# An attention and expert kernel on one core: the rounding of the expert's weights moves from POOL to DVE, and the additions for the last 64 keys move from POOL to DVE from the sixth double pair on

## The chip, the cores and the metric

The kernel runs on one core of a Trainium2 chip. The metric is the time of one execution on the device in microseconds (us); the kernel before has a median of 554.97 us over 3 runs (554.33 to 555.19). The engines are called as in the profile: PE does the matrix products and PEld loads their weights, DVE is the vector engine, ACT computes tanh and exp, POOL is the general-purpose engine (it also issues indirect DMAs), and SP issues the other DMAs.

## The reference, cut to what matters

```python
def _attn_ref(q, k, v, cap):                 # q, k, v: 8 x 12 x 448 x 64, float32
    scores = q @ k.transpose / sqrt(64)
    scores = cap * np.tanh(scores / cap)
    scores = scores - max(scores)
    attn = np.exp(scores); attn = attn / (sum(attn) + 1e-09)
    return attn @ v

def _moe_ref(x, w_gate, w1, w2, capacity):   # x: 8 x 448 x 768; w1: 768 x 1024; w2: 1024 x 768
    scores = x @ w_gate
    out = x.copy()
    for b in range(8):
        top_idx = the 128 rows of x[b] with the highest scores
        xe = x[b, top_idx]
        ye = np.maximum(xe @ w1, 0.0) @ w2
        out[b, top_idx] = xe + sigmoid(scores[b, top_idx]) * ye
```

## The kernel before

**Work and order.** Attention is done in 24 double pairs (class `Double`, number `d`, 0 to 23): four heads of one batch element, three double pairs for each of the 8. A double pair is seven steps, each 128 keys of one pair of heads, except the step `(None, 3)`, which holds the last 64 keys of both pairs: pair 0 in partitions 0 to 63 of its tile `pl`, pair 1 in partitions 64 to 127. Two steps make a block of the main loop in `fast_path`. In a block PE forms the scores of the two new steps (line 225, tile `ps`), ACT turns them into `p` or `pl` by tanh and exp (lines 241 and 242), and PE multiplies the two steps of the block before by `v` into the accumulators `x` (pair 0) and `y` (pair 1) (lines 258 and 262). On PE, ACT, DVE and POOL the instructions run in the order in which the program writes them; the SP queue is ordered by a scheduler, with the loads of `q`, `k` and `v` given a priority, and runs in that order.

**The row sums.** `e_step` adds the three 128-key tiles of a pair on DVE into `e` (lines 277 and 279) and then adds the half of `pl` that belongs to the pair, 64 partitions by 896 elements, on POOL (line 283). Once both pairs of a double pair are through, four matrix products with ones (line 291) sum `e` over the keys. DVE copies the sums to `sm` (line 294), PE transposes them (319), DVE makes the reciprocals `rec` (322, 325). `take_x` copies an accumulator to `xT` right behind `e_step` (line 270), PE transposes it (334), and DVE multiplies it by `rec` into `xn` (338), which SP stores and which DVE reduces with `w_gate` to scores (`jk`, line 351).

**Selection and expert.** After each third double pair DVE ranks the scores of the batch element (lines 381 to 421, among them line 393, which counts ties), POOL gathers the 128 chosen rows, and the expert's products (lines 505 and 525) are put between the attention blocks. The transposes of all these steps and the expert's accumulators share two banks, `pt` and `ph`. Each block runs on DVE in this order: what the block before deferred (`sm`, `rec`, `xn`), then `e_step` and `take_x`, then scores and ranking, then one step of the weights' generator.

**The weights.** The expert multiplies in split precision: each weight is a rounded part (`w1h`, `w2h`) and a rest (`w1l`, `w2l`). `weights_gen` makes them once, early in the program, in 14 chunks, 6 of w1 (128x1024) and 8 of w2 (128x768), through three staging buffers (`hs` and two called `stage`). In the kernel before, POOL rounds a chunk (line 183) and DVE subtracts one block later (line 177); the subtraction frees the buffer, and the DMA on SP that loads the next chunk into it (line 167) waits for it. A DMA issued behind it on SP waits with it.

Of the kernel before, what the change touches and what calls it, by code (L numbers as in the profile page):

```python
# [8 lines left out]
F32 = mybir.dt.float32  # L9
# [4 lines left out]
ALU = mybir.AluOpType  # L14
# [7 lines left out]
WARM = 3  # L22
BUDGET = 2500
TAIL = 1500
EVAC, SPLIT = 1300, 2200
HALF = (slice(0, HD), slice(HD, 2 * HD))

# [127 lines left out]
def weights_gen(tc, K, w1, w2):  # L155
    nc = tc.nc
    parts = [(nm, w, i, m) for nm, w, n, m in (("w1", w1, K.ND, K.F), ("w2", w2, K.NF, K.DM))
             for i in range(n)]
    staged = []

    def load(n):
        nm, w, i, m = parts[n]
        if n % 3 == 0:
            st = K.hs
        else:
            st = K.work.tile([P, 1024], F32, tag=("mh", "ml")[n % 3 - 1], name="stage", bufs=1)
        nc.sync.dma_start(st[:, :m], w[i * P:(i + 1) * P, :])
        staged.append(st)

    for n in range(3):  # L170
        load(n)
    yield
    for n in range(len(parts) + 1):
        if n:
            nm, w, i, m = parts[n - 1]
            hi, lo = K.wts[nm + "h"], K.wts[nm + "l"]
            nc.vector.tensor_tensor(lo[:, i, :], staged[n - 1][:, :m], hi[:, i, :].bitcast(F32),
                                    op=ALU.subtract)
            if n + 2 < len(parts):
                load(n + 2)  # L180
        if n < len(parts):
            nm, w, i, m = parts[n]
            nc.gpsimd.tensor_copy(K.wts[nm + "h"][:, i, :], staged[n][:, :m])
        yield


# [86 lines left out]
def e_step(tc, K, D, h, c):  # L273
    nc = tc.nc
    if c == 1:
        D.E[h] = K.work.tile([P, 2, K.S], F32, tag="E", name="e", bufs=3)
        nc.vector.tensor_tensor(D.E[h], D.P[h, 0], D.P[h, 1], op=ALU.add)  # L277
    elif c == 2:
        nc.vector.tensor_tensor(D.E[h], D.E[h], D.P[h, 2], op=ALU.add)  # L279
    if (h, c) in (D.order[3], D.order[6]):  # L280
        i = int((h, c) == D.order[6])
        e, pl = D.E[i], D.P[None, 3]
        nc.gpsimd.tensor_tensor(e[HALF[i]], e[HALF[i]], pl[HALF[i]], op=ALU.add)  # L283


def sums_mm(tc, K, D):
# [352 lines left out]
def fast_path(tc, K, first, wgen):  # L639
# [33 lines left out]
    while u <= nblocks or sums or fill.busy() or any(K.queues.values()):  # L673
# [14 lines left out]
        for s in old:  # L688
            if s:
                e_step(tc, K, *s)  # L690
                take_x(tc, K, *s)
# [13 lines left out]
        if not K.tail:  # L705
# [16 lines left out]
            if not new[0]:  # L722
                K.t += TAIL
        else:
            end = K.t + TAIL
            fill.expert(TAIL)
            K.t = max(K.t, end)
# [8 lines left out]
def main_kernel(ctx: ExitStack, tc: tile.TileContext, q, k, v, cap, w_gate, w1, w2, out, C, dims):  # L736
# [23 lines left out]
    with tc.If(fast > 0) as cmp:  # L760
        engines = {mybir.EngineType.PE, mybir.EngineType.Activation, mybir.EngineType.DVE,
                   mybir.EngineType.Pool}
        with tc.manual_schedule(engines=engines) if C <= P else nullcontext():
            fast_path(tc, K, first, weights_gen(tc, K, w1, w2))
    with cmp.Else():
        load_consts(tc, K)
        for _ in weights_gen(tc, K, w1, w2):
            pass
        general_path(tc, K)
# [47 lines left out]
```

## Time and profile before

| | |
|---|---|
| median of 3 runs | 554.97 us (554.33 to 555.19) |
| profiled execution | 556.0 us, of which 554.2 us lie between its first and its last instruction (the span) |
| PE busy | 513.5 us, 93% of the span, mean granted clock 0.988 |
| DVE busy | 352.2 us (64%) |
| ACT busy | 360.4 us (65%) |
| POOL busy | 139.2 us (25%) |

Busy time is an average over stages that are bound by different engines. Until about 98 us the weights are prepared beside the attention; from there to about 500 us attention and expert run together; the rest is the last batch element's selection and expert, one step after the other. In the profile an instruction that waits inside the engine counts as busy, so a group whose mean lies far above its least time was held up while it ran.

### The profile page before, as it was taken

The numbers are of one execution on the slowest core, as the hardware profiler recorded it, in microseconds if no ns is written. First come the engines' busy times: TensorE is split into PE (matmuls) and PEld (weight loads), VectorE is DVE, ScalarE is ACT, GpSimd is POOL, SyncE is SP. The second block draws the span as 40 slices with busy tenths as digits, with TensorE's granted clock in tenths as the row PEclk, the third lists the DMA queues.
The fourth block names the chain that finished last, engine by engine and source line by source line (L and its number), as shares of the span: only waits on it lengthen the run. The fifth ranks groups of instructions, "written<-read, shape, count | busy, mean of one in ns | idle before, by whom it ended". The sixth has DMA issues, their size and how long they took to land.

```text
span 554.2 us, 8869 instructions
## 1 busy us (share of the span) xinstructions
PE 513.5 (93%) x3446; PEld 260.4 (47%) x3446; DVE 352.2 (64%) x775; ACT 360.4 (65%) x394; POOL 139.2 (25%) x88
## 2 busy tenths in 40 slices
PE   5889989999999999999899998999999998988994
PEld 2223323354544445444454455545454454626884
DVE  1799999757636557665865565854865644865611
ACT  4987976976667574876657775686666866560110
POOL 1565532413212130431122311231313221130000
PEclk9998999999999999999999999999999999998898
DMA  7546653423214231632232331432323412212100
GB/s 256 190 156 190 193 163 119 125 86 101 74 55 149 81 100 39 186 101 84 82 108 85 114 118 34 127 130 67 99 85 107 135 47 87 67 57 69 29 30 34
DMA packets 32034, 57.63 MB, mean 104 GB/s; under 512 B 2944, under 2 KB 25984, under 8 KB 31984
## 3 DMA queue, kind: packets, MB, share of 16 engines
q1 hardware_dynamic: 30704, 50.69, 29.6%
q0 software_dynamic: 1280, 6.29, 3.4%
q8 instruction: 29, 0.48, 0.4%
q14 instruction: 21, 0.17, 0.1%
HBM read 42.81 MB, written 14.16 MB: 103 GB/s over the span
## 4 chain that ended last, share of the span: by engine, by line
PE 69%; DVE 17%; issue 5%; ACT 3%; DMA 2%; POOL 1%; POOLq 0%; DVEq 0%; SPq 0%
PE ps L225 20%; PE ph L525 9%; PE y L262 8%; PE ph L505 8%; PE x L262 8%; DVE jk L351 4%; PE pt L334 3%; PE x L258 3%; PE pt L291 3%; DVE jk L393 2%; DVE e L277 2%; DVE e L279 2%; DVE xT L270 2%; ACT p L241 2%; PE pt L472 2%
## 5 line engine op out<-in xcount | busy, mean ns | idle before, releaser
L241 ACT ACTIVATE p<-ps,sc 128x896 f32<-128x896 f32 x144 | 143.4, 996 | 73.2 <-PE ps L225 61.2
L283 POOL TENSOR_TENSOR e<-e,pl 64x896 f32<-64x896 f32 x48 | 100.5, 2093 | 288.5 <-DVE e L279 235.1
L225 PE MATMUL ps<-q,k 64*64 64x448 f32 x1344 | 150.8, 555 | 6.3 <-DMA k<-in_k 3.5
L242 ACT ACTIVATE p<-p,capc 128x896 f32<-128x896 f32 x144 | 150.2, 1043 | 4.7
L225 PEld LDWEIGHTS ps<-q,k 64*64 64x64 f32 x1344 | 43.5, 133 | 71.0 <-issue 45.8
L262 PE MATMUL y<-p,v 128*64 128x448 f32 x288 | 64.9, 556 | 0.1
L262 PE MATMUL x<-p,v 128*64 128x448 f32 x288 | 64.9, 558 | 0.0
L277 DVE TENSOR_TENSOR e<-p 128x896 f32<-128x896 f32 x48 | 59.8, 1246 | 6.6 <-ACT p L242 6.6
L279 DVE TENSOR_TENSOR e<-e,p 128x896 f32<-128x896 f32 x48 | 53.3, 1111 | 5.4 <-ACT p L242 3.8
L351 DVE CUSTOM_DVE_ANT_0 jk<-xn,wg 112x256 bf16<-112x256 f32 x96 | 51.2, 534 | 2.9
L338 DVE TENSOR_TENSOR xn<-pt,rec 112x512 f32<-112x512 f32 x39 | 26.9, 690 | 26.8 <-PE pt L334 26.2
L241 ACT ACTIVATE pl<-ps,sc 128x896 f32<-128x896 f32 x24 | 24.1, 1003 | 29.1 <-PE ps L225 28.7
L270 DVE COPY xT<-x 128x448 f32<-128x448 f32 x24 | 15.0, 623 | 39.6 <-PE x L262 25.3
L262 PEld LDWEIGHTS x<-p,v 128*64 128x64 f32 x288 | 17.7, 138 | 43.4 <-issue 31.6
L262 PEld LDWEIGHTS y<-p,v 128*64 128x64 f32 x288 | 16.3, 135 | 44.8 <-issue 31.9
L525 PE MATMUL ph<-w2h,hh 128*128 128x384 f32 x112 | 27.6, 359 | 0.0
L242 ACT ACTIVATE pl<-pl,capc 128x896 f32<-128x896 f32 x24 | 25.0, 1042 | 0.8
L505 PE MATMUL ph<-w1l,xh 128*128 128x512 f32 x84 | 25.1, 409 | 0.0
L334 PE MATMUL pt<-ident,xT 128*112 128x128 f32 x156 | 24.4, 279 | 0.7 <-DVE rec L322 0.7
L511 ACT ACTIVATE hs<-ph 128x512 f32<-128x512 f32 x14 | 8.4, 598 | 25.5 <-PE ph L505 25.3
L525 PE MATMUL ph<-w2l,hh 128*128 128x384 f32 x112 | 24.9, 345 | 0.0
L525 PE MATMUL ph<-w2h,hl 128*128 128x384 f32 x112 | 24.9, 345 | 0.0
(143 smaller groups left out, 622.6 us busy)
## 6 DMA issues: line engine op xcount, KB each, us to landing
q<-in_q SPq DMA_DIRECT2D x48, 224.0 KB, 2.6
k<-in_k SPq DMA_DIRECT2D x48, 224.0 KB, 3.2
v<-in_v SPq DMA_DIRECT2D x24, 448.0 KB, 4.1
out<-xn SPq DMA_DIRECT2D x24, 448.0 KB, 3.7
stage<-in_moe_w SPq DMA_DIRECT2D x4, 512.0 KB, 6.0
stage<-in_moe_w SPq DMA_DIRECT2D x5, 384.0 KB, 3.3
hs<-in_moe_w SPq DMA_DIRECT2D x3, 384.0 KB, 3.0
hs<-in_moe_w SPq DMA_DIRECT2D x2, 512.0 KB, 5.5
```

Of the source, the lines that this page charges most:

```text
L225: tc.nc.tensor.matmul(ps[HALF[r], j, :K.S], lhsT=kk, rhs=qq, start=True, stop=True)
L241: tc.nc.scalar.activation(p, ps[:, :, :K.S], AF.Tanh, scale=K.sc)
L242: tc.nc.scalar.activation(p, p, AF.Exp, scale=K.cap)
L262: nc.tensor.matmul(D.acc[h][HALF[j], :K.S], lhsT=D.v[:, (h * 2 + j) * 3 + c, :], rhs=p[:, j, :], start=start, stop=stop)
L277: nc.vector.tensor_tensor(D.E[h], D.P[h, 0], D.P[h, 1], op=ALU.add)
L279: nc.vector.tensor_tensor(D.E[h], D.E[h], D.P[h, 2], op=ALU.add)
L283: nc.gpsimd.tensor_tensor(e[HALF[i]], e[HALF[i]], pl[HALF[i]], op=ALU.add)
L334: nc.tensor.transpose(px[:CP, c * P:(c + 1) * P], D.xT[pair][:, c * CP:(c + 1) * CP], K.ident)
L338: nc.vector.tensor_tensor(xn[:, :, pair * P:(pair + 1) * P].rearrange("p c (h d) -> p c h d", d=K.D), px[:CP].rearrange("p (c h d) -> p c ...
L351: nc.vector.tensor_tensor_reduce(out=jk[:, :W], in0=xn[:, c, :], in1=K.wg[:, grp * W:(grp + 1) * W], scale=1.0, scalar=0.0, op0=ALU.mult, ...
L505: nc.tensor.matmul(ph[:M], lhsT=l[:, i, :M], rhs=K.wts[r][:, i, fs], start=(n == 0), stop=(n == len(ops) - 1))
L525: nc.tensor.matmul(py[:M, :HH], lhsT=l[:, i, :M], rhs=K.wts[r][:, i, ds_], start=(start and n == 0), stop=(stop and n == len(ops) - 1))
```

## The change

The rounding of the weights goes to DVE, where each chunk is now rounded and subtracted in one step of the generator, and its buffer is loaded anew in the same step, one block earlier than before. The 64-key addition of line 283 stays on POOL for the double pairs 0 to 4 and goes to DVE for 5 to 23. Behind the change the lines have other numbers: the additions 277 and 279 are lines 273 and 275, the 64-key addition is line 280, the rounding line 176, the subtraction stays line 177.

```diff
+EARLY = 5
...
-    for n in range(len(parts) + 1):
-        if n:
-            nm, w, i, m = parts[n - 1]
-            hi, lo = K.wts[nm + "h"], K.wts[nm + "l"]
-            nc.vector.tensor_tensor(lo[:, i, :], staged[n - 1][:, :m], hi[:, i, :].bitcast(F32),
-                                    op=ALU.subtract)
-            if n + 2 < len(parts):
-                load(n + 2)
-        if n < len(parts):
-            nm, w, i, m = parts[n]
-            nc.gpsimd.tensor_copy(K.wts[nm + "h"][:, i, :], staged[n][:, :m])
+    for n, (nm, w, i, m) in enumerate(parts):
+        hi, lo = K.wts[nm + "h"][:, i, :], K.wts[nm + "l"][:, i, :]
+        nc.vector.tensor_copy(hi, staged[n][:, :m])
+        nc.vector.tensor_tensor(lo, staged[n][:, :m], hi.bitcast(F32), op=ALU.subtract)
+        if n + 3 < len(parts):
+            load(n + 3)
         yield
...
-        nc.gpsimd.tensor_tensor(e[HALF[i]], e[HALF[i]], pl[HALF[i]], op=ALU.add)
+        eng = nc.gpsimd if D.d < EARLY else nc.vector
+        eng.tensor_tensor(e[HALF[i]], e[HALF[i]], pl[HALF[i]], op=ALU.add)
```

On DVE, at the start of the main loop, before the change (an arrow points from what is read to what is written):

```order
L277 TENSOR_TENSOR e<-p 128x896
L279 TENSOR_TENSOR e<-e,p 128x896
L270 COPY xT<-x 128x448
L177 TENSOR_TENSOR w1l<-hs,w1h 128x1024
L277 TENSOR_TENSOR e<-p 128x896
L177 TENSOR_TENSOR w1l<-stage,w1h 128x1024
L279 TENSOR_TENSOR e<-e,p 128x896
L270 COPY xT<-y 128x448
```

The same place after the change:

```order
L273 TENSOR_TENSOR e<-p 128x896
L176 CAST w1h<-hs 128x1024
L177 TENSOR_TENSOR w1l<-hs,w1h 128x1024
L275 TENSOR_TENSOR e<-e,p 128x896
L266 COPY xT<-x 128x448
L176 CAST w1h<-stage 128x1024
L177 TENSOR_TENSOR w1l<-stage,w1h 128x1024
L273 TENSOR_TENSOR e<-p 128x896
L176 CAST w1h<-stage 128x1024
L177 TENSOR_TENSOR w1l<-stage,w1h 128x1024
L275 TENSOR_TENSOR e<-e,p 128x896
L266 COPY xT<-y 128x448
```

A subtraction became a rounding and a subtraction, and the chain of chunks stands one block earlier among the attention's instructions.

On SP, before the change, the loads of `q` and `k` for pair 1 of the third double pair (the second pair of q and k rows here) and the weight loads around them:

```order
L207 DMA q_227<-in_q 128x448
L207 DMA k_229<-in_k 128x448
L167 DMA hs_102<-in_moe_w2 128x768
L207 DMA q_256<-in_q 128x448
L207 DMA k_258<-in_k 128x448
L167 DMA stage_376<-in_moe_w2 128x768
```

After the change:

```order
L203 DMA q_229<-in_q 128x448
L203 DMA k_231<-in_k 128x448
L168 DMA hs_102<-in_moe_w2 128x768
L168 DMA stage_336<-in_moe_w2 128x768
L203 DMA q_259<-in_q 128x448
L203 DMA k_261<-in_k 128x448
```

One more weight load stands ahead of that second pair of loads; it waits for the subtraction of the chunk behind (the fifth).

On DVE, in the ranking of the second batch element, before the change:

```order
L279 TENSOR_TENSOR e<-e,p 128x896
L386 TENSOR_SCALAR jk,rk<-row,score 112x448
L393 SCALAR_TENSOR_TENSOR jk,rk<-row,score,before 112x112
L386 TENSOR_SCALAR jk,rk<-row,score 112x448
L393 SCALAR_TENSOR_TENSOR jk,rk<-row,score,before 112x224
L294 COPY sm<-pt 128x448
...
L325 RECIPROCAL rec<-rec 112x16
L270 COPY xT<-x 128x448
```

The same place after the change:

```order
L275 TENSOR_TENSOR e<-e,p 128x896
L383 TENSOR_SCALAR jk,rk<-row,score 112x448
L390 SCALAR_TENSOR_TENSOR jk,rk<-row,score,before 112x112
L383 TENSOR_SCALAR jk,rk<-row,score 112x448
L390 SCALAR_TENSOR_TENSOR jk,rk<-row,score,before 112x224
L291 COPY sm<-pt 128x448
...
L322 RECIPROCAL rec<-rec 112x16
L280 TENSOR_TENSOR e<-e,pl 64x896
L266 COPY xT<-x 128x448
```

Here the 64-key addition stands behind `sm` and `rec`, right ahead of the copy of `x`; in the double pairs whose fourth step is in the same block as line 279, and for all pairs 1, it stands right behind the addition of line 275.

## Rows read from the trace of the kernel before

**Rows 1.** The page's first part: engine, busy us (share) xinstructions.

```profile
PE 513.5 (93%) x3446; PEld 260.4 (47%) x3446; DVE 352.2 (64%) x775; ACT 360.4 (65%) x394; POOL 139.2 (25%) x88
```

**Rows 2.** Windows: length, busy PE, PEld, DVE, ACT, POOL, then clock, DMA, GB/s.

```profile
16.50:51.20 34.70, 31.52 (x217) 9.19 (x209) 33.08 (x34) 29.59 (x32) 19.29 (x13) 0.95 0.52 163
44.00:46.00 2.00, 2.00 (x7) 0.53 (x7) 1.93 (x5) 1.97 (x3) 1.38 (x2) 0.50 0.86 221
51.20:92.80 41.60, 38.54 (x285) 14.19 (x283) 40.63 (x78) 37.19 (x38) 17.80 (x11) 1.00 0.46 145
100.00:500.00 400.00, 381.85 (x2618) 192.63 (x2610) 249.41 (x571) 274.93 (x301) 92.26 (x50) 1.00 0.31 94
```

**Rows 3.** Line 177: the subtractions of two tile kinds, ns least/median/most.

```profile
L177 DVE TENSOR_TENSOR w2l<-stage,w2h x5: 948/953/2622, 53.0 to 81.8; 128x768 fp32r<-128x768 f32 x5
L177 DVE TENSOR_TENSOR w1l<-stage,w1h x4: 1214/1218/2860, 23.6 to 46.0; 128x1024 fp32r<-128x1024 f32 x4
```

**Rows 4.** Windows of line 177 alone: length, busy DVE (count), clock, DMA, GB/s.

```profile
16.50:51.20 34.70, 13.47 (x7) 0.95 0.52 163
51.20:92.80 41.60, 10.54 (x7) 1.00 0.46 145
```

**Rows 5.** Timeline, 20 to 55 us: start, duration, engine, line, operation.

```profile
21.81 1.92 DVE L277 TENSOR_TENSOR e<-p 128x896 f32<-128x896 f32 x1
...
33.01 2.08 POOL L283 TENSOR_TENSOR e<-e,pl 64x896 f32<-64x896 f32 x1 [1.09 <-DVE e L279]
33.32 2.86 DVE L177 TENSOR_TENSOR w1l<-hs,w1h 128x1024 fp32r<-128x1024 f32 x1
...
36.21 0.33 SPq L167 DMA_DIRECT2D hs<-in_moe_w  x1
...
41.99 2.53 PE L225 MATMUL ps<-q,k 64*64 64x448 f32 x12 [2.02 <-DMA k<-in_k]
...
50.82 2.09 POOL L283 TENSOR_TENSOR e<-e,pl 64x896 f32<-64x896 f32 x1 [5.44 <-DVE e L279]
...
52.05 0.25 DVE L325 RECIPROCAL rec<-rec 112x16 f32<-112x16 f32 x1
```

**Rows 6.** Tile e, 90 to 500 us: line 279's durations, ns least/median/most.

```profile
L279 DVE TENSOR_TENSOR e<-e,p x39: 1080/1092/1094, 94.4 to 496.8; 128x896 f32<-128x896 f32 x39
```

**Rows 7.** Waits of PE, whole span: us in total, times, longest us.

```profile
PE ph L291 <- POOL e L283: 3.8, 1, 3.8
PE ps L225 <- DMA k<-in_k: 3.5, 2, 2.0
...
PE pt L319 <- DVE sm L294: 2.2, 2, 1.1
PE pt L378 <- DVE score L363: 1.9, 2, 1.0
...
PE pt L472 <- DVE sm L294: 1.2, 2, 0.6
PE ph L430 <- DVE sel L421: 1.2, 1, 1.2
```

**Rows 8.** Timeline of DVE, 134 to 138 us, in the second ranking.

```profile
134.72 2.26 DVE L393 SCALAR_TENSOR_TENSOR jk<-row,score,before 112x112 bf16<-112x112 f32 x1
...
137.50 0.44 DVE L393 SCALAR_TENSOR_TENSOR jk<-row,score,before 112x224 bf16<-112x224 f32 x1
```

**Rows 9.** Timeline of DVE, around 180 us and around 391 us.

```profile
180.37 2.34 DVE L351 CUSTOM_DVE_ANT_0 jk<-xn,wg 112x256 bf16<-112x256 f32 x1
...
182.74 0.43 DVE L351 CUSTOM_DVE_ANT_0 jk<-xn,wg 112x256 bf16<-112x256 f32 x1
...
391.11 0.62 DVE L270 COPY xT<-y 128x448 f32<-128x448 f32 x1 [0.89 <-PE y L262]
391.65 1.13 DVE L351 CUSTOM_DVE_ANT_0 jk<-xn,wg 112x256 bf16<-112x256 f32 x1
```

**Rows 10.** Timeline of POOL at 498 us, the last 64-key addition.

```profile
498.01 2.07 POOL L283 TENSOR_TENSOR e<-e,pl 64x896 f32<-64x896 f32 x1 [3.79 <-DVE e L279]
```

## The prediction, made before the changed kernel ran

> **What bounds the kernel now.** I read the page first, then the span cut into stages, then who PE waited for, and last the timeline at each of those waits. PE is busy 93% of the span, DVE 64%, POOL 25% [rows 1], so what counts is which of PE's few pauses the change shortens or lengthens. The stages differ. From 16.5 to 92.8 us, while the weights are prepared, DVE is as full as PE: 33.08 of 34.70 us and 40.63 of 41.60 us. From 100 to 500 us PE works 381.85 of 400 us and DVE only 249.41 [rows 2]. In that long stage DVE matters only at the moments at which PE stands still for one of its results: 2.2 us in two waits for the sums' copy `sm`, 1.2 us in two more behind the same copy, 1.9 us in two waits for the scores. Outside it PE waits 3.8 us once for the last 64-key addition on POOL, 1.2 us once for DVE's selection at 92 us, and 3.5 us in two waits for a load of `k` [rows 7].
>
> The second thing to see is what the two engines do to each other. A subtraction of 1024 columns takes 1.22 us and one of 768 columns 0.95 us, but some take 2.86 and 2.62 [rows 3]. The long one at 33.32 us runs beside a POOL addition that ends at 35.09 us, and it ends 1.09 us after that: it waited inside DVE. A POOL rounding does the same to an addition on DVE (1.92 us at 21.81) [rows 5], which otherwise takes 1.09 us [rows 6]. So POOL work that reads two or one tensors of SBUF holds up DVE work that reads two.
>
> **The change, step by step.** I sum against the profiled execution, 556.0 us (span 554.2 and 1.8 around it), which is 1.0 us above the median of the runs.
>
> *The weights, up to 51.2 us.* Taken off DVE's list: seven subtractions of 13.47 us together [rows 4], and what POOL's roundings cost other DVE work, 3.3 us: 0.83 us of that at 21.81 us [rows 5], the same once more, and three smaller holds of 0.5 to 0.65 us. Together 16.8 us. Put on it: by the order eight chunks instead of seven, six of 1024 and two of 768 columns, each a rounding and a subtraction. No rounding on DVE is in this trace. From above I price it as the subtraction of the same size, 1.22 and 0.95 us, and held by POOL additions as that is; from below as half of it, 0.61 and 0.48 us, since it reads one tensor and not two. I take the full price without the hold, because a one-tensor operation, the reciprocal at 52.05 us, keeps its 0.25 us beside the POOL addition that began at 50.82 us [rows 5]. Eight chunks are 6 x 2.44 + 2 x 1.90 = 18.4 us, of which about 1 us falls into a time in which DVE waited anyway. Three subtractions still find a POOL addition running, for some 0.5 us each: 18.9 us. DVE is 2.1 us later, less the 1.6 us of its idle time in the stretch, of which I let 1.0 count: about 1.0 us later at 51 us.
>
> *The weights, from 51.2 to 92.8 us.* Off: 10.54 us of subtractions [rows 4] and 2.2 us of holds of the same kind. On: six chunks of 1.90 us and two remaining holds of 0.6 us, 12.6 us. It evens out. The lateness of 1.0 us stays until 92 us, where PE already waits for DVE [rows 7], so I add **1.0 us** there. With the bounds: from below 2.2 and 2.9 us are gained, from above it costs 4.3 and 1.6 us.
>
> [...]
>
> *The loads.* The second pair of loads of `q` and `k` now stands behind one more weight load, which waits for the fifth chunk's subtraction. The old order had it behind the load at 36.21 us, which waited for the subtraction that ended at 36.18 us [rows 5]. By the prices above the fifth chunk is subtracted between 35.5 and 36.7 us, so the pause of 2.0 us at 41.99 us stays, give or take 0.7, and with it the half clock behind it (0.50 from 44 to 46 us) [rows 2]. The other wait for `k` should go, because its loads no longer queue behind a late subtraction; I price that at nothing, since DVE, not PE, leads until 92 us.
>
> *The additions from the sixth double pair on.* 38 additions of 2.1 us leave POOL, 38 of about 1.1 us come to DVE (same 896 columns as line 279 [rows 6]); 42 us more work on an engine that has 150 us idle between 100 and 500 us [rows 2]. What they hold up on DVE today goes away. The tie count that takes 2.26 us at 134.72 cannot need more than the 0.44 us of its larger neighbour [rows 8]: at least 1.8 us sooner, and since the new addition stands behind `sm` there, PE's wait for `sm` (1.1 us) goes: **1.1 us**. The same at 180.37, where a score reduction takes 2.34 instead of 0.43 us [rows 9]: **1.1 us**. At 391 us the reduction loses 0.7 us of holding, and the addition ahead of the copy of `y` mostly fits into the 0.89 us in which DVE waits for PE [rows 9]: 0.5 us of the wait for the scores, twice, **1.0 us**. Shortly behind each of those a tie count is freed as above, and the waits of 0.6 us go, twice, **1.2 us**. Elsewhere the addition stands ahead of a copy of `x` or `y`. Most of these copies wait for PE anyway; if that cover were gone, a copy would be 1.1 us later, and next in line would be the transposes of `xT` and the next products into the same accumulator, each about a block later.
>
> *The end.* The last addition, 2.07 us on POOL [rows 10], is what PE waits 3.8 us for [rows 7]. On DVE it takes 1.1 us: **1.0 us**, and from there on everything is serial.
>
> Sum: -4.4 - 1.0 + 1.0 = -4.4 us. That makes 551.6 us for the profiled execution and **550.6 us** against the median.
>
> **The rivals.**
> 1. *Roundings held by POOL.* If a rounding on DVE costs as much as a subtraction and is also locked out by the ten POOL additions that stay, DVE runs 5.9 us late by 92 us instead of 1.0, and the starved pause at 42 us grows by up to 4 us, with up to 2 us more at half clock of which I count 1. Then -5.4 + 6.9 = +1.5: 556.5 us, slower. It decides once the early stage loses more than 6.5 us. For it: DVE has no room there. Against it: the reciprocal beside POOL.
> 2. *Roundings cheap.* At half price the early stage gains 2.2 + 2.9 us, of which PE can take back what it loses there (two waits for `k`, one for the selection, 4.7 us at most): about 3.5 us, so 546.1 us. [...]
> 3. *The freed DVE time is not PE's.* In the long stage PE's next wait could take the place of the shortened one, since `pt` and `ph` are shared and ACT or the other transposes come right behind. Then perhaps 1 us is left of 4.4 and the early loss takes it: 555 us, no change.
>
> **How the numbers follow.** Forecast 0.60, with a range of its own of 548.5 to 553.5; rival 1 0.12; rival 2 0.13; rival 3 0.15. The range of 547.0 to 556.0 leaves out half of rival 2 and half of rival 1 and a little of the rest. Two runs of this kernel differ by up to 0.2%, 1.1 us, which is what I call no change. Faster: all of rival 2, nearly all of the forecast, 0.72. The same: rival 3 and a rest of the forecast, 0.16. Slower: 0.12.
>
> **What would show it.** In the changed profile the waits of PE for `sm` and the scores should shrink from 5.3 us to under 1.5, the wait ahead of the last sums from 3.8 to 2.8; the additions on DVE should take 1.1 us and the reductions near 0.43 throughout the long stage. The windows should give 16.5 to 92.8 us about the same work on DVE. The forecast is wrong if roundings beside POOL additions take over 2 us, if PE's pause at 42 us is longer than 3 us, or if copies to `xT` come to hold the products.

## The result

The changed kernel took 549.28 us (median of 5 runs, 548.88 to 550.28) against 554.97 us for the kernel before: a ratio of 0.9899, 95% interval 0.9884 to 0.9913. It is faster by 5.7 us. The profiled execution of the changed kernel took 548.9 us, with a span of 546.8 us.

**The profile after.** The first part of the page (engine, busy us, share of the span, instructions):

```profile
PE 511.7 (94%) x3446; PEld 259.1 (47%) x3446; DVE 379.2 (69%) x827; ACT 360.6 (66%) x394; POOL 43.5 (8%) x36
```

Against [rows 1], POOL has lost 96 us and DVE has gained only 27. The 38 additions alone are 41 us on DVE, and the 14 roundings some 17 more. The rest is work that DVE does faster now. The costliest groups of instructions show where (busy us, then the mean of one in ns; behind the second bar the engine's idle time ahead of them), first two of before and then those of after:

```profile
L351 DVE CUSTOM_DVE_ANT_0 jk<-xn,wg 112x256 bf16<-112x256 f32 x96 | 51.2, 534 | 2.9
L393 DVE SCALAR_TENSOR_TENSOR jk<-row,score,before 112x112 bf16<-112x112 f32 (+3 forms) x32 | 21.9, 686 | 0.0
```

```profile
L348 DVE CUSTOM_DVE_ANT_0 jk<-xn,wg 112x256 bf16<-112x256 f32 x96 | 42.6, 444 | 3.0
L280 DVE TENSOR_TENSOR e<-e,pl 64x896 f32<-64x896 f32 x38 | 41.0, 1078 | 1.0
...
L280 POOL TENSOR_TENSOR e<-e,pl 64x896 f32<-64x896 f32 x10 | 20.9, 2086 | 71.1 <-DVE e L275 61.4 <-PE x L258 9.7
...
L390 DVE SCALAR_TENSOR_TENSOR jk<-row,score,before 112x112 bf16<-112x112 f32 (+3 forms) x32 | 16.4, 512 | 0.0
```

An addition takes 1.08 us on DVE and 2.09 on POOL. A score reduction (line 348) takes 0.444 us on average, where it took 0.534, and a tie count (line 390) 0.512, where it took 0.686. Nobody changed these two; they are the work that POOL's additions held up.

The same stretches as in [rows 2]:

```profile
16.50:51.20 34.70, 32.23 (x240) 10.17 (x236) 33.97 (x42) 31.37 (x33) 8.34 (x4) 1.00 0.52 167
44.00:46.00 2.00, 2.00 (x18) 0.65 (x20) 1.90 (x7) 1.97 (x3) 0.49 (x1) 1.00 0.65 177
51.20:92.80 41.60, 37.05 (x268) 12.27 (x259) 40.54 (x81) 34.90 (x36) 10.44 (x5) 1.00 0.43 138
100.00:500.00 400.00, 386.91 (x2643) 196.65 (x2640) 275.19 (x613) 275.61 (x302) 16.34 (x13) 1.00 0.31 94
```

In the long stage PE works 386.9 of 400 us and no longer 381.85. The two windows do not hold quite the same work, since after the change 100 to 500 us reaches some 4 us further into the end; the stage is measured between two fixed instructions below. In the early stage DVE is about as full as before (74.5 us in the two windows together, 73.7 before). PE's waits, to set beside [rows 7] (us in total, times, longest):

```profile
PE pt L288 <- POOL e L280: 3.8, 3, 1.8
PE ph L288 <- DVE e L280: 2.8, 1, 2.8
...
PE pt L375 <- DVE score L360: 1.3, 2, 0.6
PE ph L427 <- DVE sel L418: 1.2, 1, 1.2
...
PE ps L221 <- DMA k<-in_k: 0.9, 1, 0.9
...
PE ph L316 <- DVE sm L291: 0.4, 1, 0.4
...
PE pt L316 <- DVE sm L291: 0.2, 1, 0.2
```

The waits for `sm` of 1.1 us are gone, and the small ones that remain lie in the early stage. The wait ahead of the last sums fell from 3.8 to 2.8 us, and one of the two waits for `k` is gone. One line has grown. Before, PE waited for POOL's additions ahead of `pt` once:

```profile
PE pt L291 <- POOL e L283: 0.5, 1, 0.5
```

Now it waits three times (1.8 us at 63.6, 1.5 at 78.5 and 0.5 us at 98.4), where DVE reaches the sums later than before.

The gain can be laid out by the start of the same PE instruction in both traces: the selection of the first batch element, and the transposes of the seventh one's scores. First before, then after:

```profile
92.31 0.77 PE L430 MATMUL ph<-vals,sel 112*128 112x4 f32 x4 [1.19 <-DVE sel L421]
469.43 0.56 PE L378 MATMUL pt<-ident,score 112*112 112x112 f32 x4 [1.42 <-DVE hl L475]
```

```profile
92.94 0.77 PE L427 MATMUL ph<-vals,sel 112*128 112x4 f32 x4 [1.21 <-DVE sel L418]
465.06 0.56 PE L375 MATMUL pt<-ident,score 112*112 112x112 f32 x4 [1.42 <-DVE hl L472]
```

The selection starts 0.63 us later, so the early stage lost that much in this pair of profiles. From there to the transposes 5.0 us are won (372.1 us in place of 377.1), and over the last sums 1.07 more. Behind them the profile of before shows half clock again, a granted clock of 0.58 from 520 to 524 us, and that of after does not (1.00). I don't count the 1.5 us that this makes to the change: the kernels below show a clock of 0.91 or of 1.00 from 512 to 530 us without a pattern that I could find, and the three terms, 5.4 us, already make up nearly all of the 5.7 between the medians.

### The profile page after: what moved, and what is told of

Same layout as the page of the kernel before. It is cut to its first block, busy times and chain, and to the rows that moved or that the text cites. A ratio compares the mean times of both kernels' runs of the same rounds, so it can differ in the third digit from the quotient of the medians.

```text
span 546.8 us, 8774 instructions
## 1 busy us (share of the span) xinstructions
PE 511.7 (94%) x3446; PEld 259.1 (47%) x3446; DVE 379.2 (69%) x827; ACT 360.6 (66%) x394; POOL 43.5 (8%) x36
## 4 chain that ended last, share of the span: by engine, by line
PE 69%; DVE 18%; issue 6%; ACT 4%; DMA 1%; POOL 0%; POOLq 0%; DVEq 0%
PE ps L221 19%; PE ph L522 10%; PE ph L502 9%; PE x L258 8%; PE y L258 8%; DVE jk L348 3%; PE pt L331 3%; PE pt L288 3%; PE x L254 2%; DVE xT L266 2%; DVE e L275 2%; ACT p L237 2%; PE pt L469 2%; DVE e L273 2%; DVE xn L335 1%
## 5 line engine op out<-in xcount | busy, mean ns | idle before, releaser
L273 DVE TENSOR_TENSOR e<-p 128x896 f32<-128x896 f32 x48 | 52.5, 1094 | 6.3 <-ACT p L238 6.2
L275 DVE TENSOR_TENSOR e<-e,p 128x896 f32<-128x896 f32 x48 | 52.2, 1088 | 2.4 <-ACT p L238 0.8
L348 DVE CUSTOM_DVE_ANT_0 jk<-xn,wg 112x256 bf16<-112x256 f32 x96 | 42.6, 444 | 3.0
L280 DVE TENSOR_TENSOR e<-e,pl 64x896 f32<-64x896 f32 x38 | 41.0, 1078 | 1.0
L438 POOL DMA_INDIRECT xe<-out,idx x8 | 10.2, 1270 | 348.4 <-DVE gt L442 348.1
L288 PE MATMUL pt<-e,ones 128*32 128x448 f32 x176 | 24.2, 551 | 3.8 <-POOL e L280 3.8
L280 POOL TENSOR_TENSOR e<-e,pl 64x896 f32<-64x896 f32 x10 | 20.9, 2086 | 71.1 <-DVE e L275 61.4
```

The source lines that it names most:

```text
L280: eng.tensor_tensor(e[HALF[i]], e[HALF[i]], pl[HALF[i]], op=ALU.add)
L288: nc.tensor.matmul(ps[32 * i:32 * i + 32, :S], lhsT=K.ones, rhs=D.E[i // 2][:, i % 2, :], start=True, stop=True)
L348: nc.vector.tensor_tensor_reduce(out=jk[:, :W], in0=xn[:, c, :], in1=K.wg[:, grp * W:(grp + 1) * W], scale=1.0, scalar=0.0, op0=ALU.mult, ...
```

## The experiments

All ratios are to the kernel before, run beside each kernel, with a 95% interval. The kernel before had medians of 554.55 to 555.35 us in these comparisons, so two rows are better compared by their ratios than by their times.

| kernel | us | ratio, interval |
|---|---|---|
| the change | 549.28 | 0.9899, 0.9884 to 0.9913 |
| roundings on DVE, all additions on POOL | 556.41 | 1.0026, 1.0014 to 1.0037 |
| roundings on POOL, additions as in the change | 548.14 | 0.9892, 0.9872 to 0.9913 |
| the same without the very last addition | 549.27 | 0.9912, 0.9891 to 0.9933 |
| the very last addition alone | 553.86 | 0.9985, 0.9971 to 0.9999 |
| the change, all additions on DVE | 551.47 | 0.9939, 0.9922 to 0.9957 |
| the same, but one addition at 96 us on POOL | 549.36 | 0.9912, 0.9894 to 0.9931 |
| the change, rounding as a maximum of two inputs | 556.40 | 1.0033, 1.0021 to 1.0045 |
| the change, rounding as a reduction over one element | 550.86 | 0.9914, 0.9897 to 0.9931 |
| additions alone, second one ahead of the full one | 550.45 | 0.9928, 0.9909 to 0.9947 |
| additions alone, another order at the end | 545.05 | 0.9825, 0.9803 to 0.9848 |

### The change taken apart

My theory: the additions carry the gain, through what they no longer hold up, and the roundings cost about 1 us. The rival: the long stage's waits only change places, and the gain is somewhere else. The first kernel has the roundings alone.

```diff
-EARLY = 5
+EARLY = 24
```

> The rounding of the weights on DVE as in the change, all 48 additions of the 64 keys on POOL. My theory: the gain is the additions' alone, and the rounding by itself loses what the changed trace shows at the end of the early stage, where the selection of the first batch element stands 0.6 us later (92.94 against 92.31 us): 555.6 us, ratio 1.001, and the waits for sm and the scores in the long stage stay at about 5 us. Rival: the rounding gives a good part of the gain, since POOL's holds of DVE's early work go, the loads of q and k come sooner and the half clock behind the pause at 42 us does not come: 551 to 552.5 us.

It took 556.41 us, by the ratio 1.4 us more than before. Its trace keeps the waits for `sm` (1.08 and 1.02 us), those for the scores and the 3.75 us ahead of the last sums, and its selection begins at 93.40 us, 1.1 us later than before. The second kernel is the kernel before with the additions alone.

```diff
-        nc.gpsimd.tensor_tensor(e[HALF[i]], e[HALF[i]], pl[HALF[i]], op=ALU.add)
+        eng = nc.vector if D.d >= 5 else nc.gpsimd
+        eng.tensor_tensor(e[HALF[i]], e[HALF[i]], pl[HALF[i]], op=ALU.add)
```

> The additions as in the change (POOL for the double pairs 0 to 4, DVE from 5 on), the rounding on POOL as before. My theory: slightly faster than the change, 548.7 us, ratio 0.9887; the selection at 92.3 us as before, the long stage about 5 us shorter, the end about 1 us. Rival: without the rounding's part 551.5 to 553 us.

It took 548.14 us. So the whole gain is the additions', and the roundings give some of it back: 1.1 us by the times of these two kernels and 0.4 by their ratios, with overlapping intervals, and 1.4 us by the kernel above. Two more kernels part the additions. The first moves the last one alone:

```diff
+        eng = nc.vector if D.d == 23 and i == 1 else nc.gpsimd
```

The second moves all from the sixth double pair on but the last one:

```diff
+        eng = nc.vector if 5 <= D.d and (D.d, i) != (23, 1) else nc.gpsimd
```

> The kernel before with only the very last addition (double pair 23, pair 1) on DVE. My theory: PE's wait ahead of the last sums falls from 3.8 to 2.8 us and all that follows moves up by 1.1 us: 553.9 us, ratio 0.998. Rival: the later work waits for something else, no change.

> The kernel before, with the 64-key additions on DVE from the sixth double pair on except the very last one, which stays on POOL; the roundings stay on POOL. Theory (the long stage carries the gain, the end about one microsecond): the additions alone ran at 548.1 us and the last one alone won 0.85 us, so about 549.1 us, a ratio of 0.990, with the last wait for the sums at 3.8 us as before and no waits of PE for sm at 138 and 184 us. Rival (half or more of the gain comes from the end, with the clock that the longer wait there costs): 551 us or more, 0.993.

They took 553.86 and 549.27 us. The last addition is worth 0.85 us by itself (its interval reaches from 0.1 to 1.6) and 1.1 with the others (intervals overlapping); the 37 ahead of it are worth 4.9 us of the gain of 6. That is the theory, and the third rival of the prediction is out.

The profiles say the same with less noise. From the first selection to the seventh batch element's transposes PE needs 377.0 to 377.1 us in the three kernels that have these additions on POOL (before, the roundings alone, the last addition alone). It needs 372.1 to 372.3 us in four that have them on DVE: the change, the additions alone, those without the last one, and the last kernel below.

The start of the selection is less steady than that. In the six kernels here with the roundings on POOL, whose POOL and DVE instructions are the same up to there, it lies between 91.33 and 92.38 us, with a mean of 91.8; in the two with the roundings on DVE and the early additions on POOL it lies at 92.94 and 93.40. So the roundings cost the early stage about 1.3 us, and the 0.63 above is one pair out of this spread.

### Why the early additions stay on POOL

> The change with all 48 additions on DVE, POOL having none. In the changed trace the ten early additions on POOL hold six roundings for 8.7 us together and some reductions for about 2 us; on DVE they cost 10 x 1.08 us. My theory: DVE's early work is the same within 1 us, and PE's waits for POOL's sums (3.8 us) shrink by about 1 us each to DVE's shorter addition: 547.5 us, 1 to 2 us faster than the change, all roundings at 0.69 and 0.55 us. Rival: DVE, full until 92 us, is 5 us later or more, since the holds are partly idle time anyway: 553 us.

```diff
-EARLY = 5
+EARLY = 0
```

It took 551.47 us: slower than the change by 2.2, and my theory missed. With POOL idle every rounding is fast, as the line of the rounding shows (ns least, median, most):

```profile
L176 DVE CAST w2h<-stage x5: 550/552/560, 48.4 to 79.7; 128x768 fp32r<-128x768 f32 x5
L176 DVE CAST w1h<-stage x4: 675/683/687, 20.2 to 37.0; 128x1024 fp32r<-128x1024 f32 x4
```

and still the kernel loses. The timeline behind the selection says where (start, duration, engine, line, operation):

```profile
96.46 1.09 DVE L280 TENSOR_TENSOR e<-e,pl 64x896 f32<-64x896 f32 x1
...
98.37 0.16 DVE L442 TENSOR_TENSOR gt<-ph,gt 128x1 f32<-128x1 f32 x1
98.56 0.20 ACT L445 ACTIVATE gt<-gt 128x1 f32<-128x1 f32 x1 [4.07 <-DVE gt L442]
98.67 0.99 ACT L237 ACTIVATE pl<-ps,sc 128x896 f32<-128x896 f32 x1
...
99.71 0.98 PE L221 MATMUL ps<-q,k 64*64 64x448 f32 x8 [1.16 <-ACT pl L237]
```

The addition stands in DVE's list ahead of the gate's small operations. ACT's gate activation waits for those, and the exponentials queue behind it in ACT, so PE waits for ACT. In the changed kernel the same activation starts at 97.02 us. To see whether this one addition is the loss or only the place where DVE's load shows, it alone goes back to POOL:

```diff
+        eng = nc.gpsimd if D.d < EARLY or (D.d, i) == (4, 1) else nc.vector
```

> All additions on DVE as in the earlier run that took 551.5 us, but the second one of the fifth double pair, at about 96 us, goes back to POOL. Theory (that one addition holds the gate's small DVE operations, ACT's gate activation waits 4.1 us for them with the next exponentials queued behind it, and PE waits 1.2 and 1.0 us for the exponentials): these two waits of PE go, and the time falls by 1.2 to 1.8 us to about 549.9 us, 0.991. Rival (the loss is DVE's load as a whole before 92 us, and the ACT waits are only where it shows): it stays at 551 us, 0.9935.

It took 549.36 us, 2.1 us less (1.5 by the ratios), level with the change within the noise. PE's two waits of 1.2 and 1.0 us behind the activation are gone, and the activation starts at 96.78 us. From the selection to the seventh batch element's transposes PE needs 372.2 us, and 373.6 with that addition on DVE. So one addition of 1.09 us, put in front of a chain that passes DVE, ACT and PE, cost 1.4 to 2.1 us; for the other nine early additions no difference between DVE and POOL shows.

### What holds a rounding up

In the change, six of the 14 roundings are long (ns least, median, most; then POOL's first addition and two roundings, of which the first ran beside it):

```profile
L176 DVE CAST w2h<-stage x5: 553/1075/2232, 49.1 to 80.3; 128x768 fp32r<-128x768 f32 x5
L176 DVE CAST w1h<-stage x4: 684/1470/2331, 18.8 to 38.1; 128x1024 fp32r<-128x1024 f32 x4
```

```profile
18.42 2.08 POOL L280 TENSOR_TENSOR e<-e,pl 64x896 f32<-64x896 f32 x1 [11.98 <-DVE e L275]
```

```profile
18.80 2.25 DVE L176 CAST w1h<-stage 128x1024 fp32r<-128x1024 f32 x1
...
23.23 0.69 DVE L176 CAST w1h<-stage 128x1024 fp32r<-128x1024 f32 x1
```

POOL's addition ends at 20.50 and the rounding at 21.05 us: it got through most of its work only when POOL was done. Without POOL beside it, it takes 0.69 us. The other five long ones also run beside a POOL addition, and with POOL idle (the kernel above with all additions on DVE) none is long. From 768 to 1024 columns a rounding takes 0.13 us more and a subtraction 0.27, and no subtraction of the change is long (0.96 and 1.23 us at most). I took the copy's faster pace to be the reason, an assumption that these numbers do not show. So I replaced the copy by a two-input operation with the same result: by that theory a rounding takes 1.22 or 0.95 us like the subtraction and none is held, and the total is 548.3 to 550.3 us.

```diff
-        nc.vector.tensor_copy(hi, staged[n][:, :m])
+        nc.vector.tensor_tensor(hi, staged[n][:, :m], staged[n][:, :m], op=ALU.max)
```

> The change, with the rounding copy on DVE replaced by the maximum of the chunk with itself, a two-input operation with the same result. [...] Rival (any DVE operation that writes these weights is held, whatever its form): roundings of 2.7 us and more beside POOL's additions, 5 us more of DVE before 92 us and 551 us or more.

It took 556.40 us, 7 us more than the change: the theory fell and the rival held. The 14 roundings take 23.7 us in place of 17.2, and the selection starts at 99.74 us, 6.8 us later than in the change. Line 176 now shows slower roundings that are held just the same:

```profile
L176 DVE TENSOR_TENSOR w2h<-stage x5: 949/1461/2626, 53.2 to 86.7; 128x768 fp32r<-128x768 f32 x5
L176 DVE TENSOR_TENSOR w1h<-stage x4: 1218/2012/2857, 19.8 to 41.2; 128x1024 fp32r<-128x1024 f32 x4
```

The subtractions of the change are short for another reason than I gave: each stands right behind a rounding that has already waited for POOL. In the kernel before, where they come first, they were held like that [rows 3]. What the theory got wrong is that two inputs protect. The next kernel reads one input, at the slower pace: a maximum over an axis of one element. I expected no rounding over 1.3 us, the rest of the hold on the subtractions behind them, and 549.3 to 551 us.

```diff
-        nc.vector.tensor_copy(hi, staged[n][:, :m])
+        nc.vector.reduce_max(hi, staged[n][:, :m].rearrange("p (f o) -> p f o", o=1), axis=mybir.AxisListType.X)
```

> [...] Rival (POOL's addition stops every DVE read of a weight chunk): roundings over 2.5 us beside it, about 555 us as with the maximum.

It took 550.86 us, and now no rounding is held, also not the one at 19.86 us, which takes 1.21 us where the change has 2.25 (at 18.80) and the maximum 2.81 (at 19.78). The subtraction behind it takes the rest of the hold, 1.57 us in place of 1.22:

```profile
L176 DVE TENSOR_REDUCE w1h<-stage x4: 1204/1207/1209, 19.9 to 37.5; 128x1024 fp32r<-128x1024 f32 x4
...
L176 DVE TENSOR_REDUCE w1h<-hs x2: 1209/1214/1219, 15.9 to 27.5; 128x1024 fp32r<-128x1024 f32 x2
```

```profile
L177 DVE TENSOR_TENSOR w1l<-stage,w1h x4: 1224/1398/1632, 21.1 to 38.8; 128x1024 fp32r<-128x1024 f32 x4
```

So of the three forms of the rounding the two-input maximum (up to 2.87 us) and the fast copy (up to 2.33) stand still beside a POOL addition, and the reduction (1.22 at most) does not. Why the copy is held and the reduction is not, the runs do not show. The unheld form is no better as a kernel: roundings and holds together take DVE 17.3 us, as in the change.

### The order at the end

PE waits 2.8 us ahead of the last sums in the additions-only kernel too. I thought of the two additions behind the last exponential and issued the 64-key one earlier, from the sixth double pair on.

```diff
-    if (h, c) in (D.order[3], D.order[6]):
-        i = int((h, c) == D.order[6])
+    if (h, c) in (D.order[3], D.order[6 if D.d < 5 else 5]):
+        i = int((h, c) != D.order[3])
...
-        nc.gpsimd.tensor_tensor(e[HALF[i]], e[HALF[i]], pl[HALF[i]], op=ALU.add)
+        eng = nc.vector if D.d >= 5 else nc.gpsimd
+        eng.tensor_tensor(e[HALF[i]], e[HALF[i]], pl[HALF[i]], op=ALU.add)
```

> The kernel before with the additions on DVE from the sixth double pair on, and of those the second one of each double pair issued a step earlier, ahead of the last full addition in place of behind it; the roundings stay on POOL. Theory (at the end PE waits for everything that DVE does behind the last exponential: a full addition of 1.09 us and a 64-key one of 1.08 us): the last wait for the sums falls from 2.8 to 1.7 us and the time from 548.1 to about 547.1 us, 0.987, with the long stage as it was. Rival (the earlier addition stands ahead of copies that PE needs, and waits for sm or the scores come back in the long stage): 548.5 us or more, 0.990.

It took 550.45 us, 2.3 more than the additions alone (2.0 by the ratios), by the rival's mechanism: PE has three new waits of 1.0 us for `xn`, which stands behind the earlier addition on DVE. The theory missed as well in its own place; the last wait is as long as ever.

```profile
PE pt L335 <- DVE xn L339: 3.0, 3, 1.0
PE ph L292 <- DVE e L279: 2.8, 1, 2.8
```

DVE's timeline of the additions-only kernel explains it:

```profile
488.91 0.56 DVE L476 TENSOR_TENSOR xl<-ph,xh 128x384 fp32r<-128x384 f32 x1 [2.33 <-ACT xh L475]
489.39 0.55 DVE L476 TENSOR_TENSOR xl<-pt,xh 128x384 fp32r<-128x384 f32 x1
489.85 1.08 DVE L277 TENSOR_TENSOR e<-p 128x896 f32<-128x896 f32 x1
490.97 1.09 DVE L279 TENSOR_TENSOR e<-e,p 128x896 f32<-128x896 f32 x1
492.09 1.09 DVE L284 TENSOR_TENSOR e<-e,pl 64x896 f32<-64x896 f32 x1
```

All three additions run back to back, and PE waits for the last of them, so their order among themselves is nothing to PE. They stand behind two splits of the gathered rows that wait for ACT, with DVE idle for 2.33 us, although the first two additions could have run in that time. In the last kernel these two are issued ahead of the splits, in the last double pair alone; nothing else differs from the additions-only kernel.

```diff
-    if (h, c) in (D.order[3], D.order[6]):
-        i = int((h, c) == D.order[6])
+    if (h, c) in (D.order[3], D.order[5 if D.d == 23 else 6]):
+        i = int((h, c) != D.order[3])
...
         for s in old:
             if s:
-                e_step(tc, K, *s)
+                if u < nblocks or s[1:] != (1, 1):
+                    e_step(tc, K, *s)
                 take_x(tc, K, *s)
         for f in q["dve2"]:
             f()
+        if u == nblocks - 1:
+            e_step(tc, K, *new[0])
```

> The additions alone (548.1 us in an earlier run: roundings on POOL, 64-key additions on DVE from the sixth double pair on), with DVE's order changed at the end only: the last double pair's first full addition and its 64-key addition stand ahead of the two splits of the gathered rows in place of behind them. Theory (DVE stood idle 2.3 us at 489 us because the splits, which wait for ScalarE, held the additions behind them; the last wait of PE for the sums, 2.8 us, is that order): the two additions run from 486.6 to 488.8 us in the idle time, the splits stay at 488.9 us, the last full addition ends near 491.1 us, PE's last wait falls to about 0.6 us and the time by 2.1 us to 546.0 us, 0.985. Rival (the splits are late by the two additions, and the first expert products behind them wait instead): the wait only changes its name, 548 us, 0.989.

It took 545.05 us, a ratio of 0.9825 (0.9803 to 0.9848), better than both kernels. The early additions use the idle time, and the splits keep their place behind ACT: this trace runs 0.93 us later here than that of the additions-only kernel, ACT's casts and the splits alike.

```profile
487.50 1.09 DVE L277 TENSOR_TENSOR e<-p 128x896 f32<-128x896 f32 x1
488.62 1.09 DVE L284 TENSOR_TENSOR e<-e,pl 64x896 f32<-64x896 f32 x1
489.84 0.56 DVE L476 TENSOR_TENSOR xl<-ph,xh 128x384 fp32r<-128x384 f32 x1
490.32 0.55 DVE L476 TENSOR_TENSOR xl<-pt,xh 128x384 fp32r<-128x384 f32 x1
490.78 1.08 DVE L279 TENSOR_TENSOR e<-e,p 128x896 f32<-128x896 f32 x1
```

```profile
491.91 0.95 PE L292 MATMUL ph<-e,ones 128*32 128x448 f32 x4 [0.51 <-DVE e L279]
```

PE's wait is 0.51 us and was 2.77. That is 2.3 us of the 3.1 between the two medians (3.7 by the ratios). In the profiles the granted clock behind the sums accounts for more: windows of the additions-only kernel, and below of this one (the clock is the third number from the end). That the order brings the full clock with it is not shown, since the clock behind an unchanged wait differs from kernel to kernel (the last section).

```profile
495.00:498.00 3.00, 3.00 (x11) 2.34 (x10) 0.43 (x2) 0.00 (x0) 0.00 (x0) 0.60 0.03 8
```

```profile
493.00:496.00 3.00, 2.76 (x17) 2.17 (x16) 0.90 (x3) 0.00 (x0) 0.00 (x0) 1.00 0.03 8
```

## Why the prediction was right, step by step

The forecast of 550.6 us holds, with a time 1.3 us lower, and three of its terms were measured by themselves. The terms of the additions are right in their mechanism; that of the early stage came out near by luck.

*The additions in the long stage, -4.4.* Measured 5.0 us in the trace and 4.9 by the kernel without the last addition. The mechanism was right: DVE's own work came free, and PE's waits for `sm` went. The size was a little low, at each of the four places. Counted by the start of the same PE instructions, up to 163 us 1.3 us were won and from there to 207 another 1.4 (I had 1.1 each). At 262 to 273 and at 391 to 402 it is 1.15 us each (I had 1.1): 0.3 of the wait for the scores, where I had 0.5, and 0.8 with the wait for `sm` behind it, where I had 0.6. So the waits for the scores did not shrink by 1.0 but by 0.6 us in all ([rows 7] has 1.9, the trace after 1.3). The sign I named for this step, under 1.5 us left of 5.3, was missed with 1.9, of which 0.6 lies in the early stage.

*The end, -1.0.* Measured 1.07 us in the trace, 0.85 and 1.1 by the two kernels. Right, but incomplete: I took the 2.8 us that would remain as the price of the additions. By the last experiment, most of it is the place of the splits in DVE's list, which the change left as it was.

*The early stage, +1.0.* Measured +0.63 at the selection in the one pair of profiles, about +1.3 over the eight profiles compared above, and 1.4 by the kernel with the roundings alone. The sum was nearly right and both of its prices wrong. I priced the 14 roundings at 1.22 and 0.95 us, 15.0 us, with 2.7 us of holds on the subtractions. They take 0.69 and 0.55 us where nothing is beside them, 8.5 us, and POOL holds them for 8.7: 17.2 us against my 17.7. The step that failed is the argument from the reciprocal, which reads one tensor: so does a rounding, and six of the 14 were held. Rivals 1 and 2 had each got one half, and their halves cancel; that the sum came out is luck. So the sign that I named as fatal, roundings of over 2 us beside POOL, did appear (2.33), and proved nothing about the total.

*The loads.* I kept the pause of 2.0 us at 42 us and the half clock behind it. The fifth chunk was subtracted when I said (it ended at 36.46 us), but the pause after the change is 0.86 us, at 40.91, and the clock from 44 to 46 us stayed at 1.00. What I missed is that neither was a fixed property of the kernel before. In the six kernels with the same early work and the roundings on POOL the pause lies between 0.62 and 2.26 us, in the two with the roundings on DVE it is 0.86 and 1.43, and only the profile of before has the half clock there; even the pause of 2.26 us, in the kernel with the last addition alone, is followed by a clock of 1.00. The other wait for `k`, near 75 us, did go: it is 1.5 to 1.8 us in those six and absent in both others. Its place was taken by the three waits of PE for POOL's early additions, 3.8 us together, which I had not seen: DVE, busier by the roundings, brings the sums to POOL later. The kernel with the roundings alone has the same three (3.8 us), the one with the additions alone two of 1.1 us together.

*Rival 3*, that the freed time is not PE's, is ruled out by the kernel that has the long stage's additions only and gains 0.9%.

## What to carry to other kernels

When work moves between POOL and DVE, price what it holds up and not only what it takes: 38 additions cost DVE 41 us and still won 6 us, 5 of them because POOL no longer stopped the score reductions and tie counts that PE waits for. An operation in front of a chain across engines can cost more than its length (one addition of 1.09 us at 96 us cost 1.4 to 2.1). Where an engine idles ahead of a wait, read what stands behind the waiting instruction in its list: two additions issued ahead of two waiting splits at the end took PE's wait from 2.8 to 0.5 us. And a pause that is read from one profile can be that execution's alone: the one at 42 us lay between 0.6 and 2.3 us in kernels that do the same work there.

## What the runs showed of the hardware

A rounding from float32 to the matmul's float32 form takes DVE 0.69 us for 1024 columns and 0.55 for 768, so 256 columns more cost it 0.13 us, half of what they cost the subtraction (1.22 and 0.95 us), and it is stopped for the rest of a POOL addition: the six that ran beside one in the change took 1.07 to 2.33 us and ended 0.4 to 0.6 us after it. The maximum of a tensor with itself is stopped as well (up to 2.87 us), though both inputs are the same tensor; a reduction over an axis of one element is not (1.20 to 1.22 us for 1024 columns, 0.94 to 0.95 for 768). In these traces the hold stands inside the instruction's duration and not as idle time ahead of it: the only idle time ahead of the change's 14 roundings is 1.6 us, for a load.

The granted clock does not follow the length of a pause alone. Behind a pause of 2.8 us ahead of the last sums it fell in the change (0.64 from 495 to 498 us) and with the additions alone (0.60), and it stayed at 1.00 from 480 to 500 us in two kernels with the same pause of 2.8 us: the one with the second addition issued earlier, and the one with a single early addition on POOL. Why is left open.
